# Loading the first activations and weights over two DMA queues, with fillers and statistics of the first segment placed anew

## The chip, the core and the metric

The kernel runs on one core of one Trainium2 chip. The metric is the device time of one execution in microseconds; where several runs are given, their median and their range. The profile is one execution; its span, from the first to the last instruction, is about 2 us shorter than the time (795.1 for 797.13 us before). Engines are called PE (matrix), PEld (PE's weight loads), DVE (vector), ACT (scalar), POOL and SP (which issues most DMAs). A suffix q (ACTq, SPq) marks an engine's sequencer, which issues DMAs.

## The reference, cut to what matters

The program is a pre-LayerNorm attention block with a compressive memory, then a gated MLP; only the first microseconds of the first block matter here.

```python
x = A_x                                   # [1, 2048, 1024] bf16
h = x + A(layernorm(x), wq, wk, wv, wo, beta)
h2 = h + B(layernorm(h), w_in, w_sp, b_sp, w_out)

# in A: 32 heads of 32, 4 segments of 512 tokens
q = xn @ wq;  k = xn @ wk;  v = xn @ wv   # 1024 x 1024 weights
# per segment: causal softmax attention, plus a read from a memory M, z
# mixed by g = sigmoid(beta); then M, z take up the segment's k and v
... 
```

Of the kernel before, what the change touches and what calls it, by code (L numbers as in the profile page):

```python
# [12 lines left out]
D = 1024  # L13
# [244 lines left out]
def bass_sequential_preLN__memory_aug_infini_attn__mixer_gmlp__prompt_kernel(  # L258
# [60 lines left out]
    RS = [cb("rs%d" % i, [128, 2], F32) for i in range(4)]  # L319
    RD = cb("rd", [128, 4, 4], F32)  # L320
    RDM = cb("rdm", [128, 4, 4], F32)
    RS0 = [cb("rs0%d" % i, [128, 1], F32) for i in range(4)]


    HNT = [tens("hnT0", [128, 8, L], BF16, 14 * K), tens("hnT1", [128, 8, L], BF16, 22 * K),
# [10 lines left out]
    OT = b1("oT", [128, NQ, L], BF16)  # L336

    b1 = Bump(110 * K, 120 * K)
    ONES = b1("ones", [128, 128], BF16)
    MEAN = [b1("mean%d" % i, [128, 1], F32) for i in range(4)]  # L340
    RB = b1("rb", [128, L], F32)
    DIAG = [b1("diag%d" % i, [128, 4, 128], BF16) for i in range(2)]
    JUNK = b1("junk", [128, D], BF16)
    b2 = Bump(134 * K, ARENA)
    ZSTG = [tens("zstg%d" % i, [128, 448], F32, (134 + 2 * i) * K) for i in range(4)]
# [29 lines left out]
    def bank(b):  # L375
        return PS[:, b, :]
# [7 lines left out]
    def next_bank():  # L384
        b = rot["banks"][rot["n"] % len(rot["banks"])]
        rot["n"] += 1
        return b
# [3 lines left out]
            pe.matmul(dst, lhs(i), rhs(i), start=(i == 0), stop=(i == n - 1))  # L391


    def x_load(tc):
        sp.dma_start(XCH[tc % 4][:], x2d[tc * 128:(tc + 1) * 128, :])

    def wcols(ap, lo, hi):
        return ap[:, lo:hi].rearrange("(c p) n -> p c n", p=128)

    for k in range(8):  # L400
        if k in (0, 1, 3, 5):
            x_load((k + 1) // 2)
        else:
            i = {2: 0, 4: 2, 6: 4, 7: 6}[k]
            sp.dma_start(WV[0][:, i:i + 2, :],
                         A_wv[i * 128:(i + 2) * 128, 0:512].rearrange("(c p) n -> p c n", p=128))
    sp.dma_start(WK[:, :, 0:256], wcols(A_wk, 0, 256))
    sp.dma_start(BETAB[:], A_beta.partition_broadcast(128))
    sp.dma_start(WQ[:, :, 0:256], wcols(A_wq, 0, 256))
    sp.dma_start(WV[1][:], wcols(A_wv, 512, D))  # L410


    pool.memset(MHALF[:], -0.5)
    dve.memset(ETMP[:], 0.0)
    act.activation(RDM[:, 0, 0:1], MHALF[:], ACTF.Exp)
    pool.iota(IOT[:], [[1, 128]], base=0, channel_multiplier=-1)
    pool.memset(V[:, :, :, 32:34], 1.0)
    pool.memset(BLK[:], 1.0)
    pool.memset(ONES[:], 1.0)
    pool.affine_select(out=BLK[:], in_=BLK[:], pattern=[[-32, 4]], compare_op=ALU.is_ge, fill=0.0, base=0,  # L420
                       channel_multiplier=1)
    pool.affine_select(out=BLK[:], in_=BLK[:], pattern=[[32, 4]], compare_op=ALU.is_ge, fill=0.0, base=31,
# [19 lines left out]
    def ln_stats(src):  # L442
        k = lnc[0] % 4
        lnc[0] += 1
        for i in range(2):
            dve.bn_stats(STATS[k][:, i, :], src[:, i * 512:(i + 1) * 512])
        dve.bn_aggr(MV[k][:], STATS[k][:])
        return k
# [31 lines left out]
    def v_out(s, tcl, half, b):  # L480
        o = V[:, tcl, 16 * half:16 * half + 16, 0:32]
        v = bank(b).rearrange("p (h d) -> p h d", d=32)
        if (s, tcl, half) == (0, 3, 0):
            dve.tensor_single_scalar(o, v, RS0[tcl][:], ALU.mult)
        else:
            act.activation(o, v, ACTF.Copy, scale=RS0[tcl][:] if s == 0 else 1.0)

    def v_mm(s, tcl, half, b, i):
        pe.matmul(bank(b), XNT[s % 2][:, i, tcl * 128:(tcl + 1) * 128], WV[half][:, i, :],
                  start=(i == 0), stop=(i == 7))  # L490
# [155 lines left out]
    def ln_tasks(src, dst, tcl):  # L646
        lnq[0].append((src, dst, tcl))
# [13 lines left out]

    def warm(k):
        for _ in range(k):
            pe.matmul(bank(7), IDENT[:], ETMP[:, 0, :], start=True, stop=True)

    def center(tc, mean, op=ALU.add):
        o = LNO[tc % 3]
        dve.tensor_single_scalar(o[:], XCH[tc][:], mean, op)
        return o
# [8 lines left out]
    def var0(k):  # L678
        pool.tensor_single_scalar(RS[k][:, 0:1], MV[k][:, 1:2], float(LN_EPS), ALU.add)

    def rstd0(tc):
        pool.tensor_tensor(RS0[tc][:], RS[tc][:, 0:1], MHALF[:], ALU.pow)

    def diag(tc):
        dve.tensor_single_scalar(DIAG[0][:, tc, :], IDENT[:], RS0[tc][:], ALU.mult)
        dve.scalar_tensor_tensor(DIAG[1][:, tc, :], IDENT[:], RS0[tc][:], DIAG[0][:, tc, :], ALU.mult, ALU.subtract)

    def pe_Th(tcl, src, e0, e1):
        pe_T(XNT[0], tcl, src, (e0, e1))

    warm(9)
    act_mean(1)
    var0(ln_stats(XCH[0]))
    c0 = center(0, MV[0][:, 0:1], ALU.subtract)
    c1 = center(1, MEAN[1][:])
    pe_Th(0, c0, dve, dve)
    pe_Th(1, c1, act, dve)
    act_mean(2)
    rstd0(0)
    var0(ln_stats(XCH[1]))  # L700
    rstd0(1)
    c2 = center(2, MEAN[2][:])
    act_mean(3)
    vb = [next_bank() for _ in range(2)]
    for i in range(4):
        for t in range(2):
            v_mm(0, t, 0, vb[t], i)
    pe_Th(2, c2, act, dve)
    c3 = center(3, MEAN[3][:])
    for i in range(4, 8):  # L710
        for t in range(2):
            v_mm(0, t, 0, vb[t], i)
    var0(ln_stats(XCH[2]))
    rstd0(2)
    pe_Th(3, c3, act, dve)
    act_var(3)
    rstd0(3)
    diag(0)
    v_out(0, 0, 0, vb[0])
    diag(1)  # L720
    diag(2)
    diag(3)
    v_out(0, 1, 0, vb[1])
    proj_v(0, 2, 0)
    gates()
    mask_g()
    bk, bq, br = next_bank(), next_bank(), next_bank()
    mm8(bank(bk), lambda i: WK[:, i, 0:128], lambda i: XNT[0][:, i, :])
    for i in range(2):
        pe.matmul(bank(br), ONES[:], DIAG[i][:].rearrange("p c n -> p (c n)"), start=(i == 0), stop=(i == 1))  # L730
    act.activation(RB[:], bank(br), ACTF.Copy)
    qk_out(0, 1, bk)
    mm8(bank(bq), lambda i: WQ[:, i, 0:128], lambda i: XNT[0][:, i, :])
    qk_out(0, 0, bq)
    for tc in range(4, 8):
        x_load(tc)
    sp.dma_start(WK[:, :, 256:D], wcols(A_wk, 256, D))
    sp.dma_start(WQ[:, :, 256:D], wcols(A_wq, 256, D))
    phi_exp(0)
    phi_max(0)  # L740
    rot["banks"] = [6, 7]

    CH = [("z2", FH + 448 * k, 448) for k in range(4)] + [("z1", 512 * k, min(512, FH - 512 * k)) for k in range(4)]

# [36 lines left out]
    for n in range(LAST + 1):  # L781
        s, c = divmod(n, NQ)
        f1, f2, f3, f4 = [], [], [], []
        if n < LAST:
            f1, f2 = [("qk", n + 1, 1)], [("qk", n + 1, 0)]
        if s == 0:
            f3 = [("v", 0, c, 1)] if c < 4 else [("v", 1, c - 4, 0)]
        elif s < NSEG - 1:
            if c < 2:
                f3, f4 = [("v", s, 2 * c, 1)], [("v", s, 2 * c + 1, 1)]  # L790
            elif c < 6:
                f3, f4 = [("wo", s - 1, c - 2, 0)], [("wo", s - 1, c - 2, 1)]
            else:
                f3, f4 = [("v", s + 1, 2 * (c - 6), 0)], [("v", s + 1, 2 * (c - 6) + 1, 0)]
        elif c < 2:
            f3, f4 = [("v", s, 2 * c, 1)], [("v", s, 2 * c + 1, 1)]
        elif c < 6:
            f3, f4 = [("wo", s - 1, c - 2, 0)], [("wo", s - 1, c - 2, 1)]
        elif c == 6:
            f3, f4 = [("z2", 0, 4, 0)], [("z2", 0, 5, 1)]  # L800
        else:
            f1, f2 = [("z2", 0, 6, 2)], [("z2", 0, 7, 3)]
            f3, f4 = [("z2", 0, 0)], [("z2", 0, 1)]

        def fill(lst):
            for u in lst:
                {"v": proj_v, "wo": wo, "qk": proj_qk, "z2": z2_group, "qmm": q_part, "qout": qk_out,
                 "vmm": v_part, "vout": v_out}[u[0]](*u[1:])

        if s < NSEG - 1 and c < 4:  # L810
            ln_tasks(XCH[c], XNT[(s + 1) % 2], c)
        if s < NSEG - 2 and c >= 4:
            x_load(4 * (s + 2) + c - 4)
        if s > 0 and c == 1:
            xr_load(4 * (s - 1))

        if n == 0:
            fill(f1)
            f1 = [("v", 0, 3, 0)]
            bq, bv = 6, 7  # L820
            f1 += [("qmm", n + 1, bq, 0, 2)]
            f2 = [("qmm", n + 1, bq, 2, 8), ("qout", n + 1, 0, bq), ("vmm", 0, 0, 1, bv, 0, 2)]
            f3 = [("vmm", 0, 0, 1, bv, 2, 8), ("vout", 0, 0, 1, bv)]
        logits(n, 0)
        fill(f1)
        if n > 0:
            pv(n - 1, range(3))
        logits(n, 1)
        if n > 0:
            pv(n - 1, (3,))  # L830
        bg_pop()
        fill(f2)
        logits(n, 2)
        if n < LAST:
            phi_exp(n + 1)
        while n == LAST and staged:
            z2_gelu(*staged.pop(0))
        fill(f3)
        if n < LAST:
            phi_max(n + 1)  # L840
        bg_pop()
        fill(f4)
        bg_pop()
        if n == 1:
            sp.dma_start(WO[:], wcols(A_wo, 0, D))
        if n in (24, 26):
            win_load((n - 24) // 2)
# [101 lines left out]
```

## The kernel before: the parts that the change and the argument touch

A recorder notes every operation with its tiles and puts the semaphore waits in; so all instructions carry the same source line, and the profile is read by tiles. Each engine is given its instructions in a fixed order, that of the program. Segment 0 is 4 chunks of 128 tokens. Its LayerNorm is split: a chunk is only centered, transposed on PE into `XNT[0]`, and projected; the factor 1/std is put in afterwards, when v and q, k leave PSUM.

```python
def x_load(tc):
    sp.dma_start(XCH[tc % 4][:], x2d[tc * 128:(tc + 1) * 128, :])

for k in range(8):            # x0 x1 wv0 x2 wv1 x3 wv2 wv3, 256 KB each, one queue
    if k in (0, 1, 3, 5):
        x_load((k + 1) // 2)
    else:
        i = {2: 0, 4: 2, 6: 4, 7: 6}[k]
        sp.dma_start(WV[0][:, i:i + 2, :], ...)
sp.dma_start(WK[:, :, 0:256], wcols(A_wk, 0, 256))
sp.dma_start(BETAB[:], A_beta.partition_broadcast(128))
sp.dma_start(WQ[:, :, 0:256], wcols(A_wq, 0, 256))
sp.dma_start(WV[1][:], wcols(A_wv, 512, D))
...
def warm(k):                  # matmuls on zeros, nobody reads the result
    for _ in range(k):
        pe.matmul(bank(7), IDENT[:], ETMP[:, 0, :], start=True, stop=True)
...
warm(9)
act_mean(1)
var0(ln_stats(XCH[0]))        # DVE: two bn_stats, one bn_aggr
c0 = center(0, MV[0][:, 0:1], ALU.subtract)
c1 = center(1, MEAN[1][:])
pe_Th(0, c0, dve, dve)        # 8 PE transposes, 2 copies out of PSUM
pe_Th(1, c1, act, dve)
...
for i in range(4):            # v of chunks 0 and 1, first half of the contraction
    for t in range(2):
        v_mm(0, t, 0, vb[t], i)
pe_Th(2, c2, act, dve)
c3 = center(3, MEAN[3][:])
for i in range(4, 8):
    for t in range(2):
        v_mm(0, t, 0, vb[t], i)
...
proj_v(0, 2, 0)
gates()
mask_g()
...                           # k and q of head group 0, 1/std broadcast over PE
for tc in range(4, 8):
    x_load(tc)
sp.dma_start(WK[:, :, 256:D], wcols(A_wk, 256, D))
sp.dma_start(WQ[:, :, 256:D], wcols(A_wq, 256, D))
```

Here `wv0` is rows 0 to 255 of the first 512 columns of wv, `wv1` the next 256 rows, and so on; a matmul `v_mm(0, t, 0, bank, i)` needs piece i // 2. After this prologue come 32 head groups, each with three rounds of logits and filler matmuls (projections of the next group) between them.

The softmax here doesn't subtract the row's maximum and nothing guards it: scores larger than these inputs give would overflow.

## Time and profile before

| | before |
|---|---|
| median of 3 runs | 796.51 us (796.43 to 796.62) |
| profiled run: time, span | 797.13 us, 795.1 us |
| PE busy | 789.9 us, 99% |
| first transposes of segment 0 on PE | 6.10 us |
| first wk matmul of group 0 | 14.04 us |
| first logits of group 2 | 33.99 us |

The last three rows are marks to compare kernels by: behind the first logits of group 2 only the next segment's LayerNorm moves (two groups later) and one background task of group 2.

The page of the kernel before, its busy time and its chain of waits (what ended last, followed backwards):

```profile
PE 789.9 (99%) x5657; PEld 378.4 (48%) x5657; DVE 379.3 (48%) x745; ACT 295.6 (37%) x347; POOL 172.1 (22%) x329
PE ps L209 96%; DMA wq<-in_A_wq_dram 2%; DMA xch<-in_A_x_dram 0%; DVE stats L209 0%; ACT junk L209 0%; DVE xnT L209 0%; DVE lno L209 0%; SPq L209 0%; ACT xnT L209 0%; DVE mv L209 0%; DVE fin L209 0%
```

PE bounds the kernel; only holes in PE can be won. The chain also names the transfer of the large part of wq, which PE meets at 30 us. The timeline of PE at the start of the kernel before; the columns are start and length in us, engine, source line, operation, tile written and tiles read, shapes, number of instructions merged, and in brackets the idle time before and what ended it:

```profile
1.74 4.02 PE L209 MATMUL ps<-etmp,ident 128*128 128x512 bf16 x9 [1.74 <-DVE ident L209]
6.10 1.14 PE L209 MATMUL ps<-ident,lno 128*128 128x128 bf16 x16 [0.34 <-DVE lno L209]
7.09 0.39 PE L209 MATMUL ps<-wv,xnT 128*128 128x512 bf16 x1
7.71 1.68 PE L209 MATMUL ps<-wv,xnT 128*128 128x512 bf16 x7 [0.23 <-ACT xnT L209]
9.68 0.62 PE L209 MATMUL ps<-ident,lno 128*128 128x128 bf16 x8 [0.29 <-DVE lno L209]
10.14 1.89 PE L209 MATMUL ps<-wv,xnT 128*128 128x512 bf16 x8
11.86 0.61 PE L209 MATMUL ps<-ident,lno 128*128 128x128 bf16 x8
12.31 1.89 PE L209 MATMUL ps<-wv,xnT 128*128 128x512 bf16 x8
14.04 1.89 PE L209 MATMUL ps<-xnT,wk 128*128 128x512 bf16 x8
...
33.99 0.40 PE L209 MATMUL ps<-qk 32*128 32x512 bf16 x4
```

The first line is warm-up work. From 9.68 us on each line begins where the one before hands over: eight 512-column matmuls take 1.73 us from start to start, 0.216 us each (12.31 to 14.04). The warm-up matmuls stood 0.427 us apart in the trace, twice that: the array still ran at half the later pace.

### The profile page before, as it was taken

The page shows a single profiled execution, that of the slowest core. Times are in us where ns is not written, and L with a number is a line of the kernel's source. Part 1 is how long each engine was busy: PE and PEld are TensorE (multiplying, and loading weights), DVE is VectorE, ACT ScalarE, POOL GpSimd, SP SyncE. Part 2 cuts the span into 40 slices and gives each one's busy share as a digit, 9 for nine tenths or more (in the row PEclk, how much of TensorE's full clock was granted, in tenths as well). Part 3 has the DMA queues.
Part 4 walks back from the last instruction along what each step waited for, and adds up shares of the span by engine and source line. Part 5 has one row for each costly group of instructions (what it writes and reads, how often), then busy time and mean ns, then how long its engine had stood idle before and what let it go on. Part 6 is the DMA issues. An engine that isn't in the chain of part 4 may idle for free.

```text
span 795.1 us, 13111 instructions
## 1 busy us (share of the span) xinstructions
PE 789.9 (99%) x5657; PEld 378.4 (48%) x5657; DVE 379.3 (48%) x745; ACT 295.6 (37%) x347; POOL 172.1 (22%) x329
## 2 busy tenths in 40 slices
PE   8999999999999999999999999999999999999998
PEld 3445455554554455455544444444444444444444
DVE  7664689679854766744562000053234323323332
ACT  5777877887787675133333333100000000000000
POOL 4564565565553331100230000000000000000000
DMA  9862555363415325411116000740270043011002
GB/s 292 181 162 57 94 81 121 87 105 84 107 23 125 114 67 139 121 47 54 54 54 132 1 1 0 222 90 7 79 133 1 33 109 78 1 59 54 1 7 86
DMA packets 125002, 64.83 MB, mean 82 GB/s; under 512 B 94992, under 2 KB 113936, under 8 KB 124944
## 3 DMA queue, kind: packets, MB, share of 16 engines
q1 hardware_dynamic: 124944, 63.99, 33.7%
q8 instruction: 44, 0.72, 0.4%
q14 instruction: 14, 0.11, 0.1%
HBM read 32.51 MB, written 8.39 MB: 51 GB/s over the span
## 4 chain that ended last, share of the span: by engine, by line
PE 96%; DMA 2%; DVE 1%; ACT 0%; SPq 0%; issue 0%
PE ps L209 96%; DMA wq<-in_A_wq_dram 2%; DMA xch<-in_A_x_dram 0%; DVE stats L209 0%; ACT junk L209 0%; DVE xnT L209 0%; DVE lno L209 0%; SPq L209 0%; ACT xnT L209 0%; DVE mv L209 0%; DVE fin L209 0%
## 5 line engine op out<-in xcount | busy, mean ns | idle before, releaser
L209 PE MATMUL ps<-wspT,z 128*128 128x512 bf16 x896 | 194.0, 379 | 0.0
L209 ACT ACTIVATE e<-ps 128x2048 bf16<-128x2048 f32 (+1 forms) x96 | 152.6, 1590 | 41.9 <-PE ps L209 41.8
L209 PEld LDWEIGHTS ps<-wspT,z 128*128 128x128 bf16 x896 | 87.7, 98 | 105.7
L209 DVE TENSOR_TENSOR tmpg<-ps,brow 128x512 f32<-128x512 f32 x56 | 38.7, 691 | 196.7 <-DMA brow<-in_B_b_sp_dram 104.0
L209 POOL TENSOR_SCALAR_AFFINE_SELECT e<-e 128x512 bf16<-128x512 bf16 x128 | 90.4, 718 | 127.2 <-ACT e L209 127.1
L209 PE MATMUL ps<-win,hnT 128*128 128x448 bf16 x512 | 98.3, 352 | 0.0
L209 PE MATMUL ps<-w_out,yT 128*128 128x512 bf16 (+2 forms) x462 | 97.4, 373 | 0.0
L209 PE MATMUL ps<-hnT,win 128*128 128x512 bf16 x448 | 96.9, 379 | 0.0
L209 PEld LDWEIGHTS ps<-win,hnT 128*128 128x128 bf16 x512 | 49.7, 98 | 46.4 <-issue 0.2
L209 PEld LDWEIGHTS ps<-w_out,yT 128*128 128x128 bf16 x462 | 44.7, 98 | 52.3
L209 PEld LDWEIGHTS ps<-hnT,win 128*128 128x128 bf16 x448 | 43.8, 98 | 52.8
L209 PE MATMUL ps<-xnT,wk 128*128 128x512 bf16 x256 | 60.8, 380 | 0.0
L209 PE MATMUL ps<-xnT,wq 128*128 128x512 bf16 x256 | 60.6, 379 | 0.1
L209 PE MATMUL ps<-wv,xnT 128*128 128x512 bf16 x256 | 59.4, 380 | 0.2 <-ACT xnT L209 0.2
L209 ACT ACTIVATE z<-ps 128x448 bf16<-128x448 f32 x60 | 32.5, 543 | 69.4 <-PE ps L209 69.4
L209 PE MATMUL ps<-wo,oT 128*128 128x512 bf16 x256 | 58.0, 379 | 0.0
L209 ACT ACTIVATE z1T<-ps 128x512 bf16<-128x512 f32 x56 | 33.4, 597 | 63.3 <-PE ps L209 63.3
L209 DVE TENSOR_TENSOR fin<-fin,ps 128x512 bf16<-128x512 bf16 (+2 forms) x33 | 22.2, 671 | 71.2 <-DMA fin<-out_dram 39.7
L209 DVE BATCH_NORM_STATS2 zst<-z 128x6 f32<-128x448 bf16 x64 | 38.9, 619 | 30.1 <-ACT z L209 30.1
L209 PEld LDWEIGHTS ps<-v,e 128*128 128x128 bf16 x1280 | 38.8, 96 | 14.0 <-issue 6.5
L209 PE MATMUL ps<-v,e 128*128 128x33 bf16 x1280 | 42.2, 178 | 0.0
L209 DVE TENSOR_TENSOR yT<-tmpg,z1T 128x512 bf16<-128x512 f32 x56 | 38.8, 692 | 1.9
(86 smaller groups left out, 609.3 us busy)
## 6 DMA issues: line engine op xcount, KB each, us to landing
xch<-in_A_x_dram SPq DMA_DIRECT2D x16, 256.0 KB, 3.3
xr<-in_A_x_dram SPq DMA_DIRECT2D x16, 256.0 KB, 3.7
out_dram<-hch SPq DMA_DIRECT2D x16, 256.0 KB, 2.4
fin<-out_dram SPq DMA_DIRECT2D x16, 256.0 KB, 2.8
out_dram<-fin SPq DMA_DIRECT2D x31, 128.0 KB, 1.7
win<-in_B_w_in_dram SPq DMA_DIRECT2D x4, 896.0 KB, 5.1
w_out<-in_B_w_out_dram SPq DMA_DIRECT2D x1, 3584.0 KB, 12.7
win<-in_B_w_in_dram SPq DMA_DIRECT2D x3, 1024.0 KB, 5.2
```

The costliest lines, as they stand in the source:

```text
L209: ins = getattr(e, op.name)(*op.args, **op.kw)
```

## The change

Its intent: get x chunks in sooner, shorten the path to the first transpose by sharing the mean of chunk 0 between ACT and DVE, free DVE of the diagonal matrices, and place fillers, gates and the next segment's LayerNorm where they hold up less. The diff, cut to its core:

```diff
-    for k in range(8):
-        if k in (0, 1, 3, 5):
-            x_load((k + 1) // 2)
-        else:
-            ...                                  # wv pieces in between, all on sp
+    x_load(0)
+    x_load(1)
+    x_load(3)
+    wv_piece(1, sp)
+    wv_piece(3, sp)
     sp.dma_start(WK[:, :, 0:256], wcols(A_wk, 0, 256))
     ...
     sp.dma_start(WV[1][:], wcols(A_wv, 512, D))
+    sp.dma_start(WK[:, :, 256:D], wcols(A_wk, 256, D))
+    sp.dma_start(WQ[:, :, 256:D], wcols(A_wq, 256, D))
 ...
+    pool.memset(XCH[2][:, 0:16], 0.0)            # holds ACT's first issue back to 1.25 us
+    x_load(2, act)
+    wv_piece(0, act)
+    wv_piece(2, act)
 ...
-            pe.matmul(bank(7), IDENT[:], ETMP[:, 0, :], start=True, stop=True)
+            pe.matmul(bank(7), ETMP[:, 0, 0:128], ETMP[:, 0, :], start=True, stop=True)
 ...
-    warm(9)
-    act_mean(1)
-    var0(ln_stats(XCH[0]))
-    c0 = center(0, MV[0][:, 0:1], ALU.subtract)
-    ...
+    warm(8)
+    act_half(0)                                  # mean of chunk 0: half on ACT,
+    dve_half(0)                                  # half on DVE
+    center_half(0, 0)
+    center_half(0, 1)
+    pe_Th(0, LNO[0], dve, dve)
+    act_mean(1)
+    vb = [next_bank() for _ in range(2)]
+    v_pair(0, 0, 2)                              # needs wv0
+    c1 = center(1, MEAN[1][:])
+    stats0(0, 0)
+    pe_Th(1, c1, dve, dve)
+    act_mean(2)
+    v_pair(0, 2, 4)                              # needs wv1
+    v_pair(1, 0, 4)
+    v_pair(0, 4, 6)
+    ...
-    gates()                                      # moved into group 0
-    mask_g()
 ...
-        if s < NSEG - 1 and c < 4:
-            ln_tasks(XCH[c], XNT[(s + 1) % 2], c)
+        if s < NSEG - 1 and 0 <= c - 2 * (s == 0) < 4:
+            t = c - 2 * (s == 0)
+            ln_tasks(XCH[t], XNT[(s + 1) % 2], t)
 ...                                              # fillers of group 0 in another order
```

The 1/std broadcast changes too: eight DVE operations on 128 x 128 diagonals and two 512-column matmuls become two tiny DVE operations and eight 128-column matmuls.

More of the change, by code (lines that the diff above doesn't have):

```diff
@@ L321, in bass_sequential_preLN__memory_aug_infini_attn__mixer_gmlp__prompt_kernel @@
     RDM = cb("rdm", [128, 4, 4], F32)
-    RS0 = [cb("rs0%d" % i, [128, 1], F32) for i in range(4)]
+    RSW = cb("rsw", [128, 4, 8], F32)
+    RS0 = [RSW[:, i, 0:1] for i in range(4)]
     HNT = [tens("hnT0", [128, 8, L], BF16, 14 * K), tens("hnT1", [128, 8, L], BF16, 22 * K),
@@ L338, in bass_sequential_preLN__memory_aug_infini_attn__mixer_gmlp__prompt_kernel @@
     b1 = Bump(110 * K, 120 * K)
-    ONES = b1("ones", [128, 128], BF16)
+    HSUM = b1("hsum", [128, 1], F32)
     MEAN = [b1("mean%d" % i, [128, 1], F32) for i in range(4)]
     RB = b1("rb", [128, L], F32)
-    DIAG = [b1("diag%d" % i, [128, 4, 128], BF16) for i in range(2)]
+    RSB = b1("rsb", [128, 2, 4], BF16)
     JUNK = b1("junk", [128, D], BF16)
@@ L391, in mm8, with x_load, wv_piece @@
             pe.matmul(dst, lhs(i), rhs(i), start=(i == 0), stop=(i == n - 1))
-    def x_load(tc):
-        sp.dma_start(XCH[tc % 4][:], x2d[tc * 128:(tc + 1) * 128, :])
+    def x_load(tc, eng=sp):
+        eng.dma_start(XCH[tc % 4][:], x2d[tc * 128:(tc + 1) * 128, :])
     def wcols(ap, lo, hi):
         return ap[:, lo:hi].rearrange("(c p) n -> p c n", p=128)
-    for k in range(8):
-        if k in (0, 1, 3, 5):
-            x_load((k + 1) // 2)
-        else:
-            i = {2: 0, 4: 2, 6: 4, 7: 6}[k]
-            sp.dma_start(WV[0][:, i:i + 2, :],
-                         A_wv[i * 128:(i + 2) * 128, 0:512].rearrange("(c p) n -> p c n", p=128))
+    def wv_piece(k, eng):
+        eng.dma_start(WV[0][:, 2 * k:2 * k + 2, :],
+                      A_wv[k * 256:(k + 1) * 256, 0:512].rearrange("(c p) n -> p c n", p=128))
+    x_load(0)
[3 more added lines that the diff above has]
+    wv_piece(3, sp)
     sp.dma_start(WK[:, :, 0:256], wcols(A_wk, 0, 256))
@@ L410, in bass_sequential_preLN__memory_aug_infini_attn__mixer_gmlp__prompt_kernel @@
     sp.dma_start(WV[1][:], wcols(A_wv, 512, D))
+    sp.dma_start(WK[:, :, 256:D], wcols(A_wk, 256, D))
+    sp.dma_start(WQ[:, :, 256:D], wcols(A_wq, 256, D))
     pool.memset(MHALF[:], -0.5)
-    dve.memset(ETMP[:], 0.0)
+    dve.memset(ETMP[:, 0, :], 0.0)
     act.activation(RDM[:, 0, 0:1], MHALF[:], ACTF.Exp)
     pool.iota(IOT[:], [[1, 128]], base=0, channel_multiplier=-1)
+    pool.memset(XCH[2][:, 0:16], 0.0)
+    x_load(2, act)
+    wv_piece(0, act)
+    wv_piece(2, act)
     pool.memset(V[:, :, :, 32:34], 1.0)
     pool.memset(BLK[:], 1.0)
-    pool.memset(ONES[:], 1.0)
     pool.affine_select(out=BLK[:], in_=BLK[:], pattern=[[-32, 4]], compare_op=ALU.is_ge, fill=0.0, base=0,
@@ L482, in v_out @@
         v = bank(b).rearrange("p (h d) -> p h d", d=32)
-        if (s, tcl, half) == (0, 3, 0):
-            dve.tensor_single_scalar(o, v, RS0[tcl][:], ALU.mult)
+        if (s, tcl, half) in ((0, 3, 0), (0, 0, 1)):
+            dve.tensor_single_scalar(o, v, RS0[tcl], ALU.mult)
         else:
-            act.activation(o, v, ACTF.Copy, scale=RS0[tcl][:] if s == 0 else 1.0)
+            act.activation(o, v, ACTF.Copy, scale=RS0[tcl] if s == 0 else 1.0)
     def v_mm(s, tcl, half, b, i):
@@ L681, in rstd0, with act_half @@
     def rstd0(tc):
-        pool.tensor_tensor(RS0[tc][:], RS[tc][:, 0:1], MHALF[:], ALU.pow)
-    def diag(tc):
-        dve.tensor_single_scalar(DIAG[0][:, tc, :], IDENT[:], RS0[tc][:], ALU.mult)
-        dve.scalar_tensor_tensor(DIAG[1][:, tc, :], IDENT[:], RS0[tc][:], DIAG[0][:, tc, :], ALU.mult, ALU.subtract)
+        pool.tensor_tensor(RS0[tc], RS[tc][:, 0:1], MHALF[:], ALU.pow)
     def pe_Th(tcl, src, e0, e1):
         pe_T(XNT[0], tcl, src, (e0, e1))
-    warm(9)
+    def act_half(tc):
+        act.activation(JUNK[:, 512:D], XCH[tc][:, 512:D], ACTF.Copy, scale=-1.0 / D, accum_out=MEAN[tc][:])
@@ new lines, in dve_half, with center_half, stats0 @@
+    def dve_half(tc):
+        dve.tensor_reduce(out=HSUM[:], in_=XCH[tc][:, 0:512], axis=mybir.AxisListType.X, op=ALU.add)
+        dve.scalar_tensor_tensor(MEAN[tc][:], HSUM[:], -1.0 / D, MEAN[tc][:], ALU.mult, ALU.add)
+    def center_half(tc, h):
+        dve.tensor_single_scalar(LNO[tc % 3][:, h * 512:(h + 1) * 512], XCH[tc][:, h * 512:(h + 1) * 512],
+                                 MEAN[tc][:], ALU.add)
+    def stats0(k, i):
+        dve.bn_stats(STATS[k][:, i, :], XCH[k][:, i * 512:(i + 1) * 512])
@@ L692, in bass_sequential_preLN__memory_aug_infini_attn__mixer_gmlp__prompt_kernel, with aggr0, v_pair @@
+    def aggr0(k):
+        dve.bn_aggr(MV[k][:], STATS[k][:])
+        var0(k)
+        rstd0(k)
+    def v_pair(t, lo, hi):
+        for i in range(lo, hi):
+            v_mm(0, t, 0, vb[t], i)
+    warm(8)
[4 more added lines that the diff above has]
+    pe_Th(0, LNO[0], dve, dve)
     act_mean(1)
-    var0(ln_stats(XCH[0]))
-    c0 = center(0, MV[0][:, 0:1], ALU.subtract)
+    vb = [next_bank() for _ in range(2)]
+    v_pair(0, 0, 2)
     c1 = center(1, MEAN[1][:])
-    pe_Th(0, c0, dve, dve)
@@ L697, in bass_sequential_preLN__memory_aug_infini_attn__mixer_gmlp__prompt_kernel @@
-    pe_Th(1, c1, act, dve)
+    stats0(0, 0)
+    pe_Th(1, c1, dve, dve)
     act_mean(2)
-    rstd0(0)
-    var0(ln_stats(XCH[1]))
-    rstd0(1)
+    v_pair(0, 2, 4)
+    v_pair(1, 0, 4)
+    v_pair(0, 4, 6)
     c2 = center(2, MEAN[2][:])
     act_mean(3)
-    vb = [next_bank() for _ in range(2)]
-    for i in range(4):
-        for t in range(2):
-            v_mm(0, t, 0, vb[t], i)
-    pe_Th(2, c2, act, dve)
-    c3 = center(3, MEAN[3][:])
-    for i in range(4, 8):
-        for t in range(2):
-            v_mm(0, t, 0, vb[t], i)
@@ L713, in bass_sequential_preLN__memory_aug_infini_attn__mixer_gmlp__prompt_kernel @@
-    var0(ln_stats(XCH[2]))
-    rstd0(2)
-    pe_Th(3, c3, act, dve)
-    act_var(3)
-    rstd0(3)
-    diag(0)
+    c3 = center(3, MEAN[3][:])
+    act_var(1)
+    rstd0(1)
+    stats0(0, 1)
+    aggr0(0)
+    pe_Th(2, c2, dve, act)
+    act_var(2)
+    rstd0(2)
+    v_pair(1, 4, 6)
+    v_pair(0, 6, 8)
+    v_pair(1, 6, 8)
+    stats0(3, 0)
+    pe_Th(3, c3, dve, act)
+    stats0(3, 1)
+    aggr0(3)
+    dve.tensor_copy(RSB[:, 0, :], RSW[:, :, 0])
+    dve.tensor_tensor(RSB[:, 1, :], RSW[:, :, 0], RSB[:, 0, :], ALU.subtract)
@@ L719, in bass_sequential_preLN__memory_aug_infini_attn__mixer_gmlp__prompt_kernel @@
+    v_out(0, 1, 0, vb[1])
     v_out(0, 0, 0, vb[0])
-    diag(1)
-    diag(2)
-    diag(3)
-    v_out(0, 1, 0, vb[1])
+    rot["n"] = 4
     proj_v(0, 2, 0)
-    gates()
-    mask_g()
-    bk, bq, br = next_bank(), next_bank(), next_bank()
+    bq, br, bk = 5, 6, 7
     mm8(bank(bk), lambda i: WK[:, i, 0:128], lambda i: XNT[0][:, i, :])
-    for i in range(2):
-        pe.matmul(bank(br), ONES[:], DIAG[i][:].rearrange("p c n -> p (c n)"), start=(i == 0), stop=(i == 1))
+    for t in range(4):
+        for h in range(2):
+            pe.matmul(PS[:, br, t * 128:(t + 1) * 128], RSB[:, h, t:t + 1].to_broadcast([128, 128]), IDENT[:],
+                      start=(h == 0), stop=(h == 1))
@@ L731, in bass_sequential_preLN__memory_aug_infini_attn__mixer_gmlp__prompt_kernel @@
     act.activation(RB[:], bank(br), ACTF.Copy)
     qk_out(0, 1, bk)
-    mm8(bank(bq), lambda i: WQ[:, i, 0:128], lambda i: XNT[0][:, i, :])
+    q_part(0, bq, 0, 8)
     qk_out(0, 0, bq)
@@ L736, in bass_sequential_preLN__memory_aug_infini_attn__mixer_gmlp__prompt_kernel @@
         x_load(tc)
-    sp.dma_start(WK[:, :, 256:D], wcols(A_wk, 256, D))
-    sp.dma_start(WQ[:, :, 256:D], wcols(A_wq, 256, D))
     phi_exp(0)
@@ L741, in bass_sequential_preLN__memory_aug_infini_attn__mixer_gmlp__prompt_kernel @@
     rot["banks"] = [6, 7]
+    rot["n"] = 0
     CH = [("z2", FH + 448 * k, 448) for k in range(4)] + [("z1", 512 * k, min(512, FH - 512 * k)) for k in range(4)]
@@ L817, in bass_sequential_preLN__memory_aug_infini_attn__mixer_gmlp__prompt_kernel @@
         if n == 0:
-            fill(f1)
-            f1 = [("v", 0, 3, 0)]
-            bq, bv = 6, 7
-            f1 += [("qmm", n + 1, bq, 0, 2)]
-            f2 = [("qmm", n + 1, bq, 2, 8), ("qout", n + 1, 0, bq), ("vmm", 0, 0, 1, bv, 0, 2)]
-            f3 = [("vmm", 0, 0, 1, bv, 2, 8), ("vout", 0, 0, 1, bv)]
+            fill([("vmm", 0, 3, 0, 7, 0, 5)])
+            f1 = [("vmm", 0, 3, 0, 7, 5, 8), ("vout", 0, 3, 0, 7)] + f1
+            f2 = [("qmm", 1, 7, 0, 8), ("qout", 1, 0, 7), ("vmm", 0, 0, 1, 6, 0, 2)]
+            f3 = [("vmm", 0, 0, 1, 6, 2, 8), ("vout", 0, 0, 1, 6)]
         logits(n, 0)
@@ L830, in bass_sequential_preLN__memory_aug_infini_attn__mixer_gmlp__prompt_kernel @@
             pv(n - 1, (3,))
-        bg_pop()
+        if n != 2:
+            bg_pop()
         fill(f2)
+        if n == 2:
+            bg_pop()
         logits(n, 2)
@@ L835, in bass_sequential_preLN__memory_aug_infini_attn__mixer_gmlp__prompt_kernel @@
             phi_exp(n + 1)
+        if n == 0:
+            gates()
+            mask_g()
         while n == LAST and staged:
@@ L843, in bass_sequential_preLN__memory_aug_infini_attn__mixer_gmlp__prompt_kernel @@
         bg_pop()
+        if n == 0:
+            rot["n"] = 1
         if n == 1:
```

## The prediction

> **What bounds the kernel now.** PE. The page gives PE 99% busy of 795.1 us and puts 96% of the chain of waits on PE. Reading the timeline of PE, from 9.7 us on the array is dense: a group of segment 0 takes 7.6 us (groups starting at 41.94, 49.54, 57.15 us), and only small holes remain: about 0.3 us before the third round of logits of group 0, 0.1 before its second, 0.28 before the wq matmuls at 30.11 (the chain names the big wq transfer, landing at 30.1), 0.1 at 41.9. All the change can win lies before about 42 us.
>
> The prologue: x chunk 0 lands at 3.8 us; statistics (two of 0.70, one of 0.21) and a centering of 0.49 on DVE delay the first transposes to 6.10. Between 6.10 and 10.14 PE has 16 transposes (0.9 us) and 8 matmuls (1.7 us at 0.215 each, start to start) to do: about 1.4 us idle. Landings, from issue time plus landing time: x1 4.4, first wv piece 6.1, x2 7.4, x3 8.8, last wv piece 10.3 us; the queue moves roughly 300 to 375 GB/s (DMA view), so 256 KB take about 0.75 us.
>
> **What changes.**
> - First chunk: half the mean on ACT, half on DVE (estimate 0.6 + 0.2), a tiny combine (0.2), then a half centering (0.28): first transposes at about 5.2 instead of 6.1 us.
> - Two queues: x3 and x2 come about 2 us sooner (5.7 and 5.4), but the first wv piece later (estimate 7.0 instead of 6.1)[...]. [...] So the total of 2 MB lands little sooner (9 to 9.5 us); order is what changes. PE will then wait for the first wv piece between 5.8 and 7.0.
> - DVE loses eight diagonal builds (2.4 us), gains two tiny ones (0.4); PE swaps 2 broadcast matmuls (0.44 us) for 8 small ones (about the same).
> - Three fewer filler matmuls before the first logits, gates and mask moved behind, LayerNorm of the next segment two groups later, big wk and wq loads ahead of x4 to x7 (1 MB, 2.7 us sooner): should remove 0.5 to 0.7 of the 0.8 us of later holes. The work itself on PE is unchanged.
>
> **Sum.** Prologue 0.3 to 1.3 us (middle 0.7), later holes 0.5 to 0.6: **795.2 us**, range **794.0 to 796.3**. Chances: faster by over 2%: 0.005; within 2%: 0.99; slower by over 2%: 0.005.
>
> **What would show it.** Timeline: first transposes near 5.2; a hole in PE until about 7.0 ended by the wv transfer; the wk matmuls of group 0 starting near 13.5 rather than 14.04; first logits near 18.6 rather than 19.75 (0.65 of that only moved filler); third group's start (33.99 before) about 1.2 us earlier; group spacing of 7.6 us unchanged; everything after 60 us shifted rigidly. Chain of waits: the wq transfer gone.
>
> **What would make it wrong.** (1) Clock: only 8 warm-up matmuls, ending near 4.7 us; before, they were still 0.427 us apart, the cold pace, at 4.70. [...] if the transposes and first matmuls run cold, up to 1 us goes. (2) ACT's DMA issues may stall as SP's do (2.2 us for betab), delaying the first half-mean. (3) The first wv piece landing at 6.3 would give 0.7 us more. (4) LayerNorm two groups later might collide on DVE in groups 2 to 5.

Three passages are cut where marked, because no trace or run shows them: the reasons for the late first wv piece, what several queues are good for, and one about the clock. 796.51 us less 0.7 and less 0.5 to 0.6 comes to 795.2 to 795.3. Beside the estimates for the first chunk stand, in the profile before, 1.06 and 0.19 us for the mean of a whole chunk on ACT and 0.49 us for its centering on DVE.

## The result, and the profile after

Four runs took 798.17 us (median; 797.71 to 799.22), against 796.57 (796.43 to 797.23) for the kernel before on the same chip. The ratio is 1.002, with a 95% interval of 1.0003 to 1.0038. A ratio here is the mean time of one kernel's fast runs over that of the other's in the same rounds, so not quite the ratio of the medians. All runs count. Two of the four list a granted clock of 0.998, two (797.71 and 797.83) list 1.000. In microseconds it is 1.6 slower where 1.3 faster had been forecast, and outside the range. The spread is also larger than before, 1.5 us against 0.8. That all four took 797.7 us or more is in part luck: the same kernel, below, had medians of 796.33 and 796.43 us.

The page after, its busy time and its chain of waits:

```profile
PE 786.1 (99%) x5570; PEld 379.2 (48%) x5662; DVE 378.6 (48%) x741; ACT 296.7 (37%) x349; POOL 166.7 (21%) x329
PE ps L209 93%; DVE stats L209 1%; DMA wv<-in_A_wv_dram 1%; DVE hch L209 1%; DVE otok L209 0%; DVE pqk L209 0%; DVE lno L209 0%; DVE ta L209 0%; DVE etmp L209 0%; DVE rd L209 0%; DVE mv L209 0%; DVE rdm L209 0%; SPq L209 0%; ACT e L209 0%; DVE upd L209 0%
```

The wq transfer is gone from the chain, as forecast, and a wv transfer has come in. (The trace misses some matmul records, 5570 beside 5662 weight loads, so busy times of PE are not compared.) The view of the cores after, with span and mean granted clock:

```profile
core 0: 796.8 us, clock 0.998
```

It had been 1.000 before. What PE waited for in the first 16 us after (total us, times, longest):

```profile
PE ps L209 <- DMA wv<-in_A_wv_dram: 2.0, 2, 1.2
```

No wait for a wv transfer was listed there before. The timeline of PE after:

```profile
1.24 3.59 PE L209 MATMUL ps<-etmp 128*128 128x512 bf16 x8 [1.24 <-DVE etmp L209]
5.12 0.87 PE L209 MATMUL ps<-ident,lno 128*128 128x128 bf16 x8 [0.28 <-DVE lno L209]
7.22 0.59 PE L209 MATMUL ps<-wv,xnT 128*128 128x512 bf16 x2 [1.23 <-DMA wv<-in_A_wv_dram]
7.65 0.61 PE L209 MATMUL ps<-ident,lno 128*128 128x128 bf16 x8
8.98 3.53 PE L209 MATMUL ps<-wv,xnT 128*128 128x512 bf16 x8 [0.72 <-DMA wv<-in_A_wv_dram]
12.30 0.71 PE L209 MATMUL ps<-ident,lno 128*128 128x128 bf16 x8
12.85 1.46 PE L209 MATMUL ps<-wv,xnT 128*128 128x512 bf16 x6
14.15 0.61 PE L209 MATMUL ps<-ident,lno 128*128 128x128 bf16 x8
...
16.32 0.38 PE L209 MATMUL ps<-xnT,wk 128*128 128x512 bf16 x1
...
35.79 0.39 PE L209 MATMUL ps<-qk 32*128 32x512 bf16 x4
```

The first transposes came at 5.12 us, as forecast. Then PE stands twice in front of a wv piece, 1.23 and 0.72 us. The line at 8.98 is the odd one: eight 512-column matmuls take 3.53 us where eight of the same shape took 1.89 at 10.14 before. (The line at 16.32 counts one matmul because the view that it is from ends at 16.5 us.) The trace records when the clock was granted; cutting the profile at those times (columns: stretch, length, busy us and instructions of PE, PEld, DVE, ACT, POOL, granted clock, DMA share, GB/s) shows:

```profile
5.68:9.09 3.41, 1.45 (x16) 0.90 (x14) 2.77 (x7) 3.27 (x7) 0.00 (x0) 1.00 1.06 327
9.09:12.50 3.41, 3.41 (x10) 1.26 (x10) 1.34 (x4) 0.83 (x2) 1.55 (x4) 0.50 1.18 297
12.50:15.91 3.41, 3.36 (x29) 2.00 (x28) 2.26 (x5) 2.84 (x6) 0.75 (x2) 1.00 1.10 351
```

The clock came up at 5.68 us, went back to half at 9.09 and up again at 12.50; the two stretches between lasted 3.41 us each. In the second the matmuls stood 0.427 us apart, behind it 0.216. In the stretch before the drop PE was busy for 1.45 us of 3.41.

The sum of the profiled pair up to the first logits of group 2 (+1.80 us, 33.99 to 35.79) can be taken apart with the traces. Up to the wk matmuls it is +2.28 (14.04 to 16.32). From the v matmuls at 8.98 to the next v matmuls at 12.85 after, PE took 3.87 us; a later trace of the same kernel in which the clock held (the second repeat below) took 2.18 for the same work (8.38 to 10.56). So 1.69 us are the clock, and the other 0.59 are what is left: the later data, net of the earlier first transposes. Behind the wk matmuls the new kernel gains 0.48 (19.95 to 19.47 us up to group 2). Together: 1.69 + 0.59 - 0.48 = 1.80.

### The profile page after: what moved, and what is told of

It is laid out like the page before. It is cut to its first block, busy times and chain, and to the rows that moved or that the text cites. A ratio compares the mean times of both kernels' runs of the same rounds, so it can differ in the third digit from the quotient of the medians.

```text
span 796.8 us, 13030 instructions
## 1 busy us (share of the span) xinstructions
PE 786.1 (99%) x5570; PEld 379.2 (48%) x5662; DVE 378.6 (48%) x741; ACT 296.7 (37%) x349; POOL 166.7 (21%) x329
## 4 chain that ended last, share of the span: by engine, by line
PE 93%; DVE 5%; issue 1%; DMA 1%; ACT 0%; SPq 0%; DVEq 0%
PE ps L209 93%; DVE stats L209 1%; DMA wv<-in_A_wv_dram 1%; DVE hch L209 1%; DVE otok L209 0%; DVE pqk L209 0%; DVE lno L209 0%; DVE ta L209 0%; DVE etmp L209 0%; DVE rd L209 0%; DVE mv L209 0%; DVE rdm L209 0%; SPq L209 0%; ACT e L209 0%; DVE upd L209 0%
## 5 line engine op out<-in xcount | busy, mean ns | idle before, releaser
L209 PE MATMUL ps<-xnT,wq 128*128 128x512 bf16 x226 | 54.0, 379 | 1.6
```

The lines of the kernel that those rows point to most:

```text
L209: ins = getattr(e, op.name)(*op.args, **op.kw)
```

## The experiments

All kernels here gave correct results. The theory: the two queues bring x first and the wv pieces late; PE, which takes its work in program order, stands in front of them (in the trace after, chunk 1 was centered at 6.91 us, but its transposes start at 7.65, behind the v matmuls that waited until 7.22); these holes also make the array's clock drop. Rivals: the second queue itself; the new statistics; the later part (collisions on DVE or POOL); only late data, no clock.

### The changed kernel again

> The changed kernel, unaltered, for its spread and for a second trace. Clock theory (two holes in PE, 1.2 and 0.7 us, in the first 9 us let the array's clock drop for about 3.4 us, which costs up to 1.7 us): times spread by over 1 us from run to run (797.7 to 799.2 so far), and where the granted clock of the run is 1.000 the time is about 1 us lower. Rival (only late data, no clock): times within 0.3 us of each other.

> The changed kernel once more. Clock theory: three kinds of runs, told by time and recorded clock: about 796.2 (clock 1.000), about 798.2 (clock 0.998: it dropped for 3.41 us after the holes), and about 797.7 (clock 1.000 but [...] the first 10 us ran slow, unrecorded, as in the trace of the run with work moved into the hole). Rival (only landing times vary): no run with clock 0.998, and times follow the landing of the first wv piece.

The first took 796.33 us (796.14 to 798.49, ratio 1.0005, interval 0.9992 to 1.0018), the second 796.43 (796.16 to 799.46, ratio 1.0004, 0.9992 to 1.0015); the first call's runs are of two kinds, the second's spread further. With the runs of the result and two looks below, 17 runs of this kernel are known: 7 took 796.1 to 796.6, 10 took 797.5 to 799.5. Six of those ten list a clock of 0.998, no other run does; half the pace for 3.41 us is 1.7 us in 797, which is that 0.2%. In one call the two runs with 0.998 (798.05 and 798.49) stand 2.0 us above the mean of the three with 1.000. Four of the slow runs list 1.000, two of them in the result; what they were is open (one reading under the work-in-the-hole run). In the second no run lists 0.998, as the rival had it, and its 799.46, the longest of all 17, lists 1.000. So the clock theory accounts for six of the ten. The rival "landing times only" falls by the first, and by the three of the six that were profiled: all three traces show the drop.

### The old loads on one queue

```diff
-    x_load(0)
-    x_load(1)
-    x_load(3)
-    wv_piece(1, sp)
-    wv_piece(3, sp)
+    x_load(0); x_load(1); wv_piece(0, sp); x_load(2)
+    wv_piece(1, sp); x_load(3); wv_piece(2, sp); wv_piece(3, sp)
 ...
-    pool.memset(XCH[2][:, 0:16], 0.0)
-    x_load(2, act)
-    wv_piece(0, act)
-    wv_piece(2, act)
```

> The changed kernel with the first loads in the order and on the one queue of before. Theory (order of the loads makes the holes, holes make the clock drop): no hole over 0.5 us after the first transposes, wk matmuls of group 0 start near 13.7 us, first transposes stay near 5.1; time 795.0 to 795.8. Rival (the new statistics and the split of the first chunk cost the time): stays at 797.5 or more.

> The one-queue kernel again, on the chip of this call: 795.3 to 796.1 in each run, 0.6 to 1.0 us under the kernel before; no clock of 0.998.

Measured 795.70 us (795.28 to 796.04; ratio 0.9988, interval 0.9975 to 1.0000), and on another chip 795.44 (795.31 to 795.99; ratio 0.9985, 0.9973 to 0.9997), against 796.53 and 796.71 before. All ten runs list a clock of 1.000. The timeline of PE of the first of these:

```profile
5.04 0.66 PE L209 MATMUL ps<-ident,lno 128*128 128x128 bf16 x8 [0.55 <-DVE lno L209]
5.96 0.60 PE L209 MATMUL ps<-wv,xnT 128*128 128x512 bf16 x2 [0.26 <-DVE xnT L209]
6.69 0.62 PE L209 MATMUL ps<-ident,lno 128*128 128x128 bf16 x8
7.62 2.01 PE L209 MATMUL ps<-wv,xnT 128*128 128x512 bf16 x8 [0.31 <-DMA wv<-in_A_wv_dram]
9.46 0.61 PE L209 MATMUL ps<-ident,lno 128*128 128x128 bf16 x8
```

With the loads alone undone the change wins 0.8 to 1.3 us, where 1.3 had been forecast (the first of the two intervals touches 1, the second does not). So the harm sits in the loads; the new statistics and the later part are sound.

### Only the later part, on the kernel before

The fillers of group 0, gates and mask later, LayerNorm two groups later, and the large wk and wq loads ahead of x4 to x7, all put into the kernel before; its prologue stays.

> The kernel before with only the part of the change behind the prologue (fillers of group 0, gates and mask later, LayerNorm two groups later, large wk and wq loads first). From the traces: wk of group 0 to first logits of group 2 took 19.95 us before and 19.47 after, so this part should win 0.5 us: 796.0. Rival (this part costs time, by DVE or POOL collisions): 796.5 or more.

Measured 796.21 us (795.98 to 796.77) against 796.53; ratio 0.9996, interval 0.9983 to 1.0010. In the trace the wk matmuls stand at 13.51 and the logits of group 2 at 32.99: 19.48 us, 0.47 less than the 19.95 before. The interval holds 1, so the medians alone show nothing; the trace shows the 0.5. This trace also has the prologue of the kernel before, and there the first transposes stood at 5.65 us and wk at 13.51, both about 0.5 us earlier than in the trace that the prediction had read: x0 landed at 3.38 instead of 3.83 us.

### Dummy matmuls in the holes

```diff
+    warm(5)
     v_pair(0, 0, 2)
     c1 = center(1, MEAN[1][:])
     ...
     act_mean(2)
+    warm(3)                                      # only in the first of the two
     v_pair(0, 2, 4)
```

> The changed kernel with 5 and 3 dummy matmuls in the two holes, nothing else: the wv pieces come when they came. Clock theory: no matmul of 0.43 us spacing after 9 us, wk matmuls of group 0 start near 14.7 instead of 16.3, time 796.2 to 796.8, narrow spread. Rival (late data alone): wk start unchanged to 0.3 us, time stays at about 798.

> The changed kernel with 5 dummy matmuls (1.1 us) in the first hole only; none in the second, where they overshot. Clock theory: no run with recorded clock 0.998; most runs 796.0 to 796.6, those where the first wv piece lands late up to 797.3. Rival: as the changed kernel, with about two runs of five at 798 or more.

The first measured 797.16 us (796.29 to 797.50), the second 796.93 (796.08 to 797.37). No run of the ten lists 0.998, none exceeds 797.5, and in neither trace do v matmuls stand 0.427 us apart; the wk matmuls start at 15.13 and 15.19 us (16.32 in the result, 14.7 expected). But the medians lie above those of the undisturbed changed kernel, 796.33 and 796.43, against what I had expected. In both traces the first wv piece landed late, at 7.83 and 8.50 us, where four traces with these loads and no dummies (the result, the two repeats, and the work-in-the-hole run below) had 6.7 to 7.3; and in the first the second set of dummies ran beyond its hole, from 8.85 to 9.49, while the piece had landed at 9.05. Whether dummies delay transfers was open, so four looks (one profile each; of such single runs the state is unknown) were taken on one chip:

> The changed kernel, a further trace: first wv piece between 6.6 and 8.0 us. Clock theory: if the time is 797.5 or more, the trace shows 0.427 us spacing of v matmuls, either from the start (missed warm-up) or from about 9 us for 3.4 us (drop).

> The changed kernel, one more trace, with the same two readings: first wv piece between 6.6 and 8.0 us, and 0.427 us spacing of v matmuls in it if the time is 797.5 or more.

> Dummies in the first hole, two queues. Chance theory: first wv piece anywhere between 6.6 and 8.5 us, as without dummies. Rival (dummies delay transfers): 7.8 us or later again.

> The one-queue kernel with the same 5 dummies where it has no hole. Chance theory: first wv piece at 5.1 to 6.0 us as in the one-queue traces; the dummies overshoot by 0.5 to 1 us, time about 796.2. Rival (dummies delay transfers): first wv piece at 6.5 us or later.

The changed kernel took 799.17 and 798.27 us; the dummies in the first hole 797.08; the one-queue kernel with dummies 795.75; the kernel before 796.63 on that chip. The first wv piece landed at 8.66 and 7.74 without dummies, 8.20 with them, and 6.24 on one queue with dummies. Both slow runs show the drop, as the clock theory had it. Landings as late as 8.66 come without dummies, so lateness does not need them. Whether dummies add to it is not settled: before, the trace with dummies had the later piece (7.83 against 6.79, 8.50 against 6.67); here it lies between the two without; and the one-queue run missed its expected 6.0 by 0.24 (its x1 had landed late as well, at 5.57 us, just as the first dummy began). Either way the looks give a pair: same chip, similar landings, with and without dummies. First the changed kernel, in two fences: the timeline of PE, then the stretches cut where its trace records a change of the clock. Behind it the kernel with dummies in the same two views, its first stretch beginning at its recorded rise of the clock:

```profile
7.88 0.59 PE L209 MATMUL ps<-wv,xnT 128*128 128x512 bf16 x2 [1.91 <-DMA wv<-in_A_wv_dram]
8.31 0.77 PE L209 MATMUL ps<-ident,lno 128*128 128x128 bf16 x8
8.87 3.45 PE L209 MATMUL ps<-wv,xnT 128*128 128x512 bf16 x8
```

```profile
5.19:8.61 3.42, 1.39 (x16) 0.98 (x17) 2.16 (x6) 3.24 (x5) 0.00 (x0) 1.00 1.00 329
8.61:12.02 3.41, 3.41 (x14) 1.46 (x12) 2.41 (x6) 1.45 (x4) 1.44 (x4) 0.50 1.19 305
```

```profile
5.74 1.24 PE L209 MATMUL ps<-etmp 128*128 128x512 bf16 x5
8.33 0.59 PE L209 MATMUL ps<-wv,xnT 128*128 128x512 bf16 x2 [1.35 <-DMA wv<-in_A_wv_dram]
8.76 0.61 PE L209 MATMUL ps<-ident,lno 128*128 128x128 bf16 x8
9.21 1.93 PE L209 MATMUL ps<-wv,xnT 128*128 128x512 bf16 x8
```

```profile
5.42:8.83 3.41, 2.06 (x17) 1.00 (x16) 1.75 (x4) 3.15 (x6) 0.00 (x0) 1.00 1.02 329
8.83:12.24 3.41, 3.36 (x28) 1.92 (x28) 3.02 (x8) 1.93 (x5) 1.31 (x4) 1.00 1.18 303
```

The second kernel starts its v matmuls 0.45 us later and ends 1.2 us sooner: its eight matmuls take 1.93 instead of 3.45 us. The dummies do no useful work; in this pair the clock holds with them (1.00 from 8.83 to 12.24 us, against 0.50 from 8.61 to 12.02). Over all runs none of the eleven with dummies on two queues lists 0.998, against six of the 17 without (about 3% likely by chance, an estimate from these counts). The slow runs are shorter with them, 796.8 to 797.5 us against 797.5 to 799.5, while the share at 796.6 or less is no larger, 3 of 11 against 7 of 17.

### What the two queues did: order or queue

```diff
 # order of landing, on one queue
+    x0 x2 x1 wv0 x3 wv2 wv1 wv3        (all on sp)
 # need order, on one queue
+    x0 x1 wv0 wv1 x2 x3 wv2 wv3        (all on sp)
 # two queues, need order
+    x0 x1 x2 x3 wv2 wv3                (sp)
+    wv0 wv1                            (act, held back to 1.25 us as before)
```

> The changed kernel with one queue only, issued in the order in which its two queues landed: x0, x2, x1, wv 0, x3, wv 2, wv 1, wv 3. Order theory: holes of about 1 us and 0.5 us as with two queues, first v matmuls near 6.5 us, fast runs near 796.2, some at 798. Queue theory (the second queue does the damage): as fast as the one-queue kernel, 795.7.

> The changed kernel with one queue in the order in which PE asks: x0, x1, wv 0, wv 1, x2, x3, wv 2, wv 3. Theory: the last 0.3 us hole of the one-queue kernel goes; wk matmuls of group 0 start near 13.1 us; 795.3 to 795.6, no run over 797. Rival (the order of the loads is not what counts): equal to the one-queue kernel, 795.7, or worse since chunk 2 comes later.

> The changed kernel with two queues: all x chunks and wv 2, 3 on SP's, wv 0 and 1 on ScalarE's. Order theory: first wv piece near 5.2 us, second near 6.7, chunk 1 near 5.2 (later than the 4.2 of one queue[...]); wk matmuls of group 0 near 13.2 to 13.5; 795.4 to 795.8, no 798. Queue theory: 796.2 or more with some 798s.

On one chip, kernel before 796.87 us: the order of landing on one queue took 796.77 (796.50 to 797.75; ratio 1.0004, interval 0.9990 to 1.0017), with waits for wv of 0.57 and 0.40 us in its trace (the first fence below), and one of 0.38 for chunk 1, whose x came third. The need order on one queue took 795.79 (795.58 to 795.96; ratio 0.9986, 0.9974 to 0.9999). Two queues with wv0 and wv1 first on ACT's took 795.61 (795.31 to 797.52; ratio 0.9988, 0.9976 to 1.0001; the second fence).

```profile
6.63 0.59 PE L209 MATMUL ps<-wv,xnT 128*128 128x512 bf16 x2 [0.57 <-DMA wv<-in_A_wv_dram]
7.61 0.62 PE L209 MATMUL ps<-ident,lno 128*128 128x128 bf16 x8 [0.38 <-DVE lno L209]
8.63 1.90 PE L209 MATMUL ps<-wv,xnT 128*128 128x512 bf16 x8 [0.40 <-DMA wv<-in_A_wv_dram]
```

```profile
6.02 0.61 PE L209 MATMUL ps<-wv,xnT 128*128 128x512 bf16 x2 [0.26 <-DVE xnT L209]
7.72 1.90 PE L209 MATMUL ps<-wv,xnT 128*128 128x512 bf16 x8 [0.36 <-DMA wv<-in_A_wv_dram]
```

So a good order on two queues is about as fast as on one, and a bad order on one queue costs about 1 us: the order of the loads counts, and a cost of the second queue as such is not shown. Two caveats. The run of 797.52 with two queues was not profiled, nor were the two slowest of the bad order (797.59 and 797.75), while none of the 15 runs in a good order on one queue exceeds 796.1; so a rare loss with two queues is not excluded. And no run of the bad order on one queue lists 0.998: there wv0 landed at 6.49, sooner than the 6.7 to 8.7 of the changed kernel, and its holes were smaller (0.57, 0.38 and 0.40 us; PE was busy for 2.15 us of the 3.41 from 6.15 on).

My idea that the need order would beat the old one (795.7) failed: in its trace the wait for wv1 is gone, but 0.21 us for wv2 and 0.16 for the later statistics have come in its place.

### Other work in the first hole

```diff
-    v_pair(0, 0, 2)
     c1 = center(1, MEAN[1][:])
     stats0(0, 0)
     pe_Th(1, c1, dve, dve)
     act_mean(2)
+    v_pair(0, 0, 2)
+    v_pair(1, 0, 2)
     v_pair(0, 2, 4)
-    v_pair(1, 0, 4)
+    v_pair(1, 2, 4)
     v_pair(0, 4, 6)
```

> The changed kernel, loads untouched, but PE transposes chunk 1 before its first v matmuls and then takes two pieces' worth of both chunks (0 and 1) from the first wv piece before it asks for the second piece. Theory (an in-order PE stands in front of late wv pieces with other work behind it): the hole at the second piece vanishes, wk matmuls of group 0 start near 13.6 us, time 795.8 to 796.1, and fewer runs of 798 or more. Rival (the second queue itself costs, whatever PE does): 796.2 with some 798s as before.

Measured 796.53 us (796.09 to 797.57; ratio 0.9999, interval 0.9986 to 1.0012), with two runs at 797.5: inconclusive as a remedy. Its trace, of a run of 797.53 us, has no hole at the second piece any more, as expected, but wk matmuls at 15.32 us instead of 13.6, and shows another way to lose time. The timeline of PE:

```profile
4.91 1.03 PE L209 MATMUL ps<-ident,lno 128*128 128x128 bf16 x8
7.25 1.03 PE L209 MATMUL ps<-ident,lno 128*128 128x128 bf16 x8 [1.31 <-DVE lno L209]
8.07 3.49 PE L209 MATMUL ps<-wv,xnT 128*128 128x512 bf16 x10
```

The hole of 1.31 us was a wait for chunk 1 itself: its x landed at 5.43 us, and ACT and DVE had it centered only at 7.20, so the work moved forward was not ready to fill the hole. (In the result's trace chunk 1 was centered at 6.91, 0.17 us before wv0 landed.) The transposes take 1.03 us each time instead of 0.61 to 0.66 at the full pace, and the ten v matmuls take 3.33 us from 8.07 to the next transposes at 11.40, where ten at 0.216 us would take 2.16 and ten at 0.427 us 4.27. So the pace had not come up with the eight warm-up matmuls; by these numbers it came up near 10.4 us (an estimate), and the first recorded change, to 1.000, is at 10.44. The run still lists a clock of 1.000. So a listed 1.000 doesn't rule out a slow start, and the four unexplained slow runs of the changed kernel may be of this kind or may just have had late data; without their traces this is not settled.

### The clock alone, with the data on time

```diff
 # the one-queue kernel
-    warm(8)
+    warm(2)
```

> The one-queue kernel (no holes over 0.4 us) with 2 instead of 8 warm-up matmuls. Clock theory: the array stays at the slow pace through the first transposes and first v matmuls, up to some time between 7 and 10 us; 0.427 us between matmuls there; 0.8 to 2 us longer than the one-queue kernel (796.5 to 797.7). Rival (warm-up does little here): within 0.3 us of 795.7.

Measured 796.44 us (796.39 to 797.41) against 795.44 for the one-queue kernel with 8 warm-ups on the same chip: 1.0 us for the slow pace, at the same loads. The timeline of PE, and one stretch of it:

```profile
5.06 1.04 PE L209 MATMUL ps<-ident,lno 128*128 128x128 bf16 x8 [2.79 <-DVE lno L209]
6.19 1.03 PE L209 MATMUL ps<-wv,xnT 128*128 128x512 bf16 x2
```

```profile
5.00:8.00 3.00, 2.84 (x19) 1.90 (x20) 2.42 (x7) 1.67 (x4) 0.00 (x0) 1.00 0.97 333
```

Two v matmuls take 1.03 us where 0.59 to 0.60 is usual, yet the column of the granted clock says 1.00. This trace holds no record of the clock at all, and the view prints 1.00 where there is none (in the profile before, which holds none either, it prints 1.00 for 1.74 to 5.58 us, where the warm-up matmuls stand 0.427 us apart), so it says nothing of a slow pace that lasts from the start.

The best kernels found are the changed one with its loads in a good order, on one queue (the old order or the need order) or on two. Their medians, 795.4 to 795.8 us, do not tell them apart; they lie about 1 us, or 0.1%, under the kernel before.

## Why the prediction was wrong, point by point

- **What bounds the kernel, and that all gain lies before 42 us:** right.
- **First transposes near 5.2 us:** right, 5.12.
- **"PE will then wait for the first wv piece between 5.8 and 7.0":** right in kind and nearly in size (7.22 in the profiled run; 6.8 to 8.8 in other traces of the same kernel). I had reckoned with ACT's first issue at 2.3 us (an estimate: in the profile before, ACT's table load and a first small operation end at 2.28); the timeline of ACT shows otherwise:

```profile
0.79 1.28 ACT L209 ACT_TABLE_LOAD   x1 [0.79 <-PEq L972]
1.25 0.39 ACTq L209 DMA_DIRECT2D xch<-in_A_x_dram  x1
```

  Its queue issued at 1.25 us, while the table load ran (0.79 to 2.07). This brought x2 in at 4.84 us, but the two wv pieces that PE asks for first came later than before (7.08 for 6.08, 8.94 for 8.12), and only the last two earlier (8.73 for 9.54, 9.62 for 10.32).
- **The step that failed first: "Prologue 0.3 to 1.3 us", a gain.** The sum had a wait for the first piece only. The second piece, wv1, landed at 8.94 us (8.12 before), and PE stood in front of it as well. Late data cost 0.59 us net in the profiled pair, in place of a gain of 0.7.
- **The step that failed most: risk (1), "up to 1 us", and its cause.** I looked for a missed warm-up. In the three traces that dropped the clock had come up (recorded rise at 5.19 to 5.68 us) and then fell behind holes of 1.23 and 0.72, of 1.91 and of 2.92 us: 1.69 us of time in the profiled pair. This accounts for six of the ten slow runs; the other four are open. The forecast had seen the hole of 1.2 us and had given it only its own length.
- **Baseline:** the holes were read from a profiled run that was 0.6 us above the median, and subtracted from the median. Part of the 1.4 us of idle time before 10.14 was a late x0 in that one execution; in another trace of the same prologue the wk matmuls stood 0.5 us earlier. Even runs of the changed kernel with no drop (796.1 to 796.6) gain only some 0.3 us.
- **Later holes, 0.5 to 0.6:** right by the traces, 0.47 and 0.48.
- **Risk (2), ACT's issues stalling:** did not happen (0.39 to 0.49 us each). **Risk (3), the first wv piece at 6.3 us:** did not happen (7.08). **Risk (4), collisions on DVE in groups 2 to 5:** none that costs; the shift at the end (795.1 to 796.8 us of span) is that at group 2 to 0.1 us.

That the whole of the first loads would land little sooner held in the profiled pair: the first 2 MB had landed at 10.32 us on one queue and at 9.62 on two (9.3 to 10.3 and 9.0 to 10.6 over all traces read). What changed is which piece came when.

## What to carry to other kernels

Order the first loads by when PE, in program order, asks for each piece, not by what other engines could start on; in the changed kernel the second queue let other pieces go ahead of the one that PE needed next, which then landed later and at times that varied more (6.7 to 8.7 us over nine traces, against 5.1 to 6.2 over seven on one queue in the old or the need order). A hole in PE early in a kernel can cost more than its length: here the clock fell where PE had been busy for 1.45 us or less of the 3.41 us after its recorded rise (0.49, 1.39 and 1.45 us in three traces, all of the changed kernel), and held at 1.64 or more (1.64, 2.01, 2.06, 2.15, 2.36, 2.47, 3.00 and 3.41 us in eight). The longest hole did not part them: the trace with 1.64 us held behind a hole of 1.97, longer than in two of the three that fell. That is what eleven traces show, and no more. With the same eight warm-up matmuls from 1.24 us on the first recorded rise came anywhere from 4.02 to 6.40 us, once at 10.44, and six of the 18 traces record no change at all. So look at the pace of the matmuls after the hole, and at the spread of the runs, not just at the idle time. And before taking gains from one trace, compare that execution's own time with the median.
